# A gate group ahead of the last unit's transposes, and three value weight units behind the token mixes

## The chip, the cores and the metric

The kernel runs on one core of a Trainium2 chip. The metric is the device time of one execution in microseconds; several executions are taken and their median is compared.

## What is computed

Three layers run one after the other: hashed attention, a gated feed-forward block with token shift, and a spatial gating block. Cut to what matters:

```
q_bucket, k_bucket = bits of (q @ proj > 0), (k @ proj > 0)       # 2 x 8 heads, 768 tokens, 64 wide
scores = where(q_bucket == k_bucket, q @ k.T / 8, -1e9)
x = softmax(scores) @ v                                            # heads side by side: 2 x 768 x 512

xk = mu_k * x + (1 - mu_k) * x_prev                                # x_prev: one token earlier
xr = mu_r * x + (1 - mu_r) * x_prev
k = relu(xk @ w_k);  r = sigmoid(xr @ w_r)
x = r * (k * k @ w_v)                                              # w_k 512x1024, w_v 1024x512, w_r 512x512

h = relu(x @ w_in);  u, v = halves of h
out = (u * (w_spatial @ layernorm(v) + b_spatial)) @ w_out
```

The change touches only the order in which the end of the attention and the first half of the second layer are issued.

## The kernel before

**Attention.** Two heads form a pair, eight pairs in all. A *unit* is one strip of 128 queries of one head: its scores (`scores`, L326, 128x768), the clamped copy and row maximum on VectorE (`peak`, L336), the exponential on ScalarE (`expo`, L354), and then `move` for each half: three transposes on TensorE (L364) and the evacuation into PT on ScalarE (L370). There are 96 units. `av3` multiplies PT by v (L399), and `finish` scales the sum on VectorE by the reciprocals (L411), which `recip` and `spread` take through two small DMAs on the SP queue (L385, L392). Three units form a step p, 32 steps in all.

**Mixers.** The second layer works on four blocks of 384 tokens. For block n, `mix_jobs` makes each of four channel slots from x and x shifted: a product `d` (L144 on ScalarE, or L146 on VectorE), a sum `f` on VectorE (L150), a rounded half on ScalarE (L121), and the remainder on VectorE or POOL (L122). Every operand is held in two parts, so a product is three matmuls. `mm3` (L176) makes a *group*: four channels by three matmuls, 12 matmuls of 128x384. `r_group(n, m)` is one gate group with its sigmoid; four make r(n). `step_k` makes eight key groups (relu, square and split on ScalarE, remainder on VectorE, L600). `step_v` multiplies them by the value weights, chunk after chunk for block 0. The order is r(0), k(0), r(1), r(2), r(3), v(0), k(1), v(1) and so on.

**Weights.** A weight unit is 128 rows by 512 columns; it comes by DMA into one of two staging buffers (`w_raw`, L37) as 64-bit words and is turned into two parts by eight jobs: magnitude (ScalarE, L41), clamp, shift, top (VectorE, L44, L49, L55), first (ScalarE, L71), power, low (VectorE, L62, L65), and rest (two instructions on VectorE for the value weights, L76 and L77). w_v has eight units.

**What sets the order.** The order on each engine is written out by the program. In the attention, jobs hang on the places of a step. From the last steps on there are *turns*: `tick()` is called after each group (and once for four pieces of `step_v`) and issues the jobs planned for that turn. Turn 0 is the first gate group; k(0) has turns 4 to 11, r(1), r(2) and r(3) turns 12 to 23, and v(0) begins behind. `plan_weight(n, ...)` puts a unit's load at turn n - 2 and its jobs at turns n to n + 3. Value units 0 and 1 begin in the attention, and only their last jobs have turns. The mixes of block 1 have turns 4 to 8, those of block 2 turns 11 to 14, of block 3 turns 15 to 18. An engine works strictly in its own order, so a job that has to wait holds up all behind it.

Of the kernel before, what the change touches and what calls it, by code (L numbers as in the profile page):

```python
# [82 lines left out]
def hash_attention_moe_kernel(  # L83
# [134 lines left out]
    with tc.manual_schedule():  # L218
        attention(**env)
        mixers(**env)  # L220


def attention(tc, nc, mid, dram, ident, msc, omu, misc, cst_sb, pb, epsT, kq, vP, XT, TK0, wr, w_r, wk,
              w_k, w_v, ps_s, ps_t, obank, mix_jobs, r_group, tick, now, at_tick, plan_weight, wv, **_):
    PS = bass.MemoryType.PSUM
    with ExitStack() as ctx:
# [89 lines left out]
        def scores(i):  # L316
            g, u = divmod(i, 6)
            pp, half = divmod(g, 2)
            e, j = divmod(u, 3)
            t = TK[pp % 2][e]  # L320
            q0 = half * HS + 128 * j
            s = ps_s.tile([128, 2, 512], F32, tag="s", name="s")
            for n in range(2):
                w = t[:, 3 - n, q0:q0 + 128]
                for c in range(2):
                    nc.tensor.matmul(  # L326
                        s[:, c, :HS], w, t[:, n, c * HS:(c + 1) * HS],
                        start=(n == 0), stop=(n == 1),
                    )
            S_ps[i] = s  # L330
# [16 lines left out]
        def expo(i):  # L347
            g, u = divmod(i, 6)
            c, nb = C_sb.pop(i)
            if u == 0:  # L350
                den[g] = at.tile([128, 6], F32, tag="den", bufs=2, name="den")
                PT[g] = mid.tile([128, 2, 6, HS], F32, tag="PT", bufs=2, name="PT")
            c = c.rearrange("p c n -> p (c n)")
            nc.scalar.activation(  # L354
                c, c, AF.Exp, bias=nb, scale=0.125, accum_out=den[g][:, u:u + 1]
            )
            P[i] = c

        def transp(i, c):
            p = P[i] if c == 0 else P.pop(i)  # L360
            t = ps_t.tile([128, 512], F32, tag="t", name="t")
            for n in range(3):
                k0 = 128 * (3 * c + n)
                nc.tensor.transpose(t[:, 128 * n:128 * n + 128], p[:, k0:k0 + 128], ident)  # L364
            return t

        def evac(i, c, t):
            g, u = divmod(i, 6)
            e, j = divmod(u, 3)
            nc.scalar.copy(  # L370
                PT[g][:, e, 3 * c:3 * c + 3, 128 * j:128 * j + 128],
                t[:, :HS].rearrange("p (n q) -> p n q", n=3),
            )
# [3 lines left out]
        def recip(g):  # L377
            rc = rcs[g % 2]
            nc.vector.tensor_scalar_add(rc[:, 0:6], den.pop(g), 1e-9)
            nc.vector.reciprocal(rc[:, 0:6], rc[:, 0:6])  # L380
            rt = at.tile([128, 32], F32, tag="rt", bufs=2, name="rt")
            nc.vector.transpose(rt, rc)
            ds = dram.tile([6, 128], F32, tag="ds", name="ds")
            for n in range(4):
                nc.sync.dma_start(ds[:, 32 * n:32 * n + 32], rt[32 * n:32 * n + 6, :])  # L385
            R[g] = ds

        def spread(g):
            ds = R[g]
            R[g] = at.tile([128, 3, 128], F32, tag="rb", bufs=2, name="rb")  # L390
            for e in range(2):
                nc.sync.dma_start(  # L392
                    R[g][64 * e:64 * e + 64],
                    ds[3 * e:3 * e + 3].unsqueeze(0).to_broadcast([64, 3, 128]),
                )
# [11 lines left out]
        def finish(g):  # L407
            pp, half = divmod(g, 2)
            b, p = divmod(pp, NP)
            PT.pop(g)  # L410
            nc.vector.tensor_mul(  # L411
                XT[:, p, b, 1 + half * HS:1 + (half + 1) * HS],
                obank[:, :HS],
                R.pop(g).rearrange("p n q -> p (n q)"),
            )
# [3 lines left out]
        early = {}  # L419
# [15 lines left out]
        def plan_wv():  # L435
            for h in range(2):
                wv.append(mid.tile([128, 2, 4, DM], F32R, tag="PT", bufs=2, name="wv"))
                for c in range(4):
                    n = 4 * h + c
                    if n < 2:  # L440
                        at_tick(n, early[n][4])
                        at_tick(n + 1, early[n][7])
                        continue
                    plan_weight(
                        (20 * n) // 7 - 2, (wv[h][:, 0, c, :], wv[h][:, 1, c, :]),
                        w_v[128 * n:128 * n + 128],
                    )

# [61 lines left out]
        def av3(p):  # L510
            for n in range(3):
                av(p // 2, 3 * (p % 2) + n)

        def move(i, c):
            evac(i, c, transp(i, c))

        def score(i):
            peak(i)
            bias(i)

        for p in range(np3):
            a = 3 * p
            scores(a)
            scores(a + 1)
            score(a)
            if a:
                move(a - 1, 0)
            expo(a)
            if a:
                move(a - 1, 1)  # L530
            score(a + 1)
            expo(a + 1)
            if p >= 3:
                av3(p - 3)
            if p >= 2 and p % 2 == 0:
                recip(p // 2 - 1)
            for job in plan.pop((p, 0), ()):
                job()
            if p >= 3 and p % 2:
                spread((p - 3) // 2)  # L540
            if p >= np3 - 2:
                tick()
            scores(a + 2)
            move(a, 0)
            move(a, 1)
            score(a + 2)
            expo(a + 2)
            if p >= 4 and p % 2 == 0:
                finish((p - 4) // 2)
            move(a + 1, 0)  # L550
            move(a + 1, 1)
            for job in plan.pop((p, 1), ()):
                job()
            if p == np3 - 2:
                plan_wv()
            if p >= np3 - 2:
                tick()
        move(nunits - 1, 0)
        move(nunits - 1, 1)
        av3(np3 - 3)  # L560
# [1 line left out]
            for job in plan.pop((np3, k), ()):  # L562
                job()
        recip(np3 // 2 - 1)
        r_group(0, 0, mid)
        finish(np3 // 2 - 2)
        r_group(0, 1, mid)
        spread(np3 // 2 - 1)
        av3(np3 - 2)
        av3(np3 - 1)  # L570
# [309 lines left out]
```

## Time and profile before

| | |
|---|---|
| median of 3 runs | 573.2 us (572.47 to 573.58) |
| profiled execution | 572.43 us, span 570.7 us |
| TensorE busy | 548.7 us, 96% of the span |
| VectorE busy | 378.0 us, 66% |
| ScalarE busy | 336.4 us, 59% |
| POOL busy | 143.2 us, 25% |
| mean granted TensorE clock | 0.988 of full speed |

Times in the profile are microseconds from the start of the span. TensorE is busy nearly all the time; a share of busy time says nothing of whether it ran at full clock, so the row of granted clock is read beside it.

### The profile page before, as it was taken

How to read it: one execution, taken by the hardware profiler on the slowest of the kernel's cores; microseconds unless marked ns; L12 is line 12 of the kernel's file. 1: busy time of each engine (PE TensorE's matmuls, PEld its weight loads, DVE VectorE, ACT ScalarE, POOL GpSimd, SP SyncE). 2: the span in 40 equal slices, each digit the busy share in tenths (PEclk: the TensorE clock that was granted, in tenths of full speed). 3: DMA queues.
4: the chain of work that ended last, by engine and by line, in shares of the span. 5: the costliest groups of instructions: out<-in, count | busy, mean ns of one | idle time of the engine just before them, and what ended most of it. 6: DMA issues, size and time to landing. Idle time of an engine off the chain costs nothing.

```text
span 570.7 us, 8997 instructions
## 1 busy us (share of the span) xinstructions
PE 548.7 (96%) x3188; PEld 468.0 (82%) x3188; DVE 378.0 (66%) x812; ACT 336.4 (59%) x718; POOL 143.2 (25%) x152
## 2 busy tenths in 40 slices
PE   7899999999999998799899999999999999999997
PEld 5676767667667765589799999999999889899996
DVE  6678887888688989439974676423997785353230
ACT  2987978798888887539754564808534453221121
POOL 5766663858293822200000000000110000000000
PEclk9999999999999999799899999999999999999999
DMA  8993589393939220202220121000473100001102
GB/s 171 240 223 87 157 152 221 86 237 78 235 90 211 76 89 14 89 0 75 74 75 2 37 74 37 2 1 0 127 253 119 51 33 1 2 14 43 55 20 92
DMA packets 20477, 51.96 MB, mean 91 GB/s; under 512 B 3840, under 2 KB 6864, under 8 KB 20432
## 3 DMA queue, kind: packets, MB, share of 16 engines
q1 hardware_dynamic: 13952, 31.71, 17.9%
q0 software_dynamic: 6336, 19.66, 16.9%
q8 instruction: 25, 0.41, 0.3%
q14 instruction: 20, 0.16, 0.1%
q10 hardware_dynamic: 144, 0.02, 0.0%
HBM read 47.08 MB, written 3.19 MB: 88 GB/s over the span
## 4 chain that ended last, share of the span: by engine, by line
PE 76%; DVE 14%; ACT 5%; issue 3%; DMA 2%; SPq 0%; POOL 0%; DVEq 0%; ACTq 0%; POOLq 0%
PE o L176 11%; PE o L399 9%; PE t L364 8%; PE v L634 8%; PE s L326 8%; PE k L176 7%; PE s L176 7%; PE w L176 5%; PE u L176 5%; PE r L176 4%; DVE p L336 4%; PE o L634 3%; DVE w_a L65 2%; ACT p L354 2%; DVE f L150 2%
## 5 line engine op out<-in xcount | busy, mean ns | idle before, releaser
L336 DVE TENSOR_SCALAR_CACHE_REDUCE p<-s 128x768 f32<-128x768 f32 x96 | 91.6, 954 | 26.9 <-PE s L326 24.2
L354 ACT ACTIVATE p<-p,nb 128x768 f32<-128x768 f32 x96 | 90.4, 942 | 18.8 <-DVE nb L344 18.5
L370 ACT COPY PT<-t 128x384 f32<-128x384 f32 x192 | 84.0, 475 | 19.9 <-PE t L364 18.9
L326 PE MATMUL s<-tk 128*128 128x384 f32 x384 | 84.8, 354 | 4.3 <-DVE p L336 2.2
L364 PE MATMUL t<-ident,p 128*128 128x128 f32 x576 | 80.4, 279 | 8.4 <-ACT p L354 5.7
L326 PEld LDWEIGHTS s<-tk 128*128 128x128 f32 x384 | 63.7, 188 | 24.3 <-issue 4.9
L364 PEld LDWEIGHTS t<-ident,p 128*128 128x128 f32 x576 | 65.6, 142 | 20.4 <-ACT p L354 10.1
L399 PE MATMUL o<-PT,v 128*64 128x384 f32 x384 | 70.7, 506 | 0.0
L176 PE MATMUL k<-tk,wk 128*128 128x384 f32 x336 | 59.6, 334 | 0.0
L258 POOL TENSOR_TENSOR tk<-x,tk 64x384 fp32r<-64x384 f32 x56 | 58.9, 1077 | 2.3 <-DMA tk<-in_kq_dram 0.8
L176 PEld LDWEIGHTS k<-tk,wk 128*128 128x128 f32 x336 | 58.4, 188 | 0.0
L634 PE MATMUL v<-k,wv 128*128 128x384 f32 x288 | 53.8, 335 | 0.6 <-DVE k L600 0.6
L634 PEld LDWEIGHTS v<-k,wv 128*128 128x128 f32 x288 | 50.3, 188 | 0.9 <-DVE k L600 0.9
L399 PEld LDWEIGHTS o<-PT,v 128*64 128x64 f32 x384 | 25.2, 139 | 29.6 <-issue 28.2
L693 POOL DMA_DIRECT2D wsp<-in_w_spT_dram x6 | 3.6, 612 | 179.0 <-DVE w_a L44 172.5
L176 PE MATMUL r<-tk,wr 128*128 128x384 f32 x168 | 34.3, 361 | 2.3 <-DVE tk L122 1.7
L176 PEld LDWEIGHTS r<-tk,wr 128*128 128x128 f32 x168 | 31.8, 204 | 5.5 <-DVE tk L122 2.3
L176 PE MATMUL o<-wk,tk 128*128 128x512 f32 (+1 forms) x168 | 36.2, 374 | 0.0
L176 PEld LDWEIGHTS o<-wk,tk 128*128 128x128 f32 x168 | 30.0, 188 | 5.5
L615 ACT ACTIVATE kr<-k 128x384 f32<-128x384 f32 x28 | 13.6, 487 | 33.0 <-PE k L176 32.8
L600 DVE TENSOR_TENSOR k<-kt,k 128x384 fp32r<-128x384 f32 x32 | 17.8, 555 | 22.2 <-ACT k L618 22.0
L176 PE MATMUL w<-wk,tk 128*128 128x512 f32 x132 | 30.7, 390 | 0.0
(108 smaller groups left out, 846.4 us busy)
## 6 DMA issues: line engine op xcount, KB each, us to landing
tk<-in_kq_dram POOLq DMA_DIRECT2D x32, 384.0 KB, 9.4
x<-in_kq_dram POOLq DMA_DIRECT2D x6, 768.0 KB, 6.6
w_raw<-in_w_k_dram SPq DMA_DIRECT2D x8, 512.0 KB
w_raw<-in_w_v_dram SPq DMA_DIRECT2D x8, 512.0 KB
w_raw<-in_w_in_dram SPq DMA_DIRECT2D x8, 512.0 KB
v<-in_vP_dram SPq DMA_DIRECT2D x8, 384.0 KB
rb<-ds SPq DMA_DIRECT2D x32, 96.0 KB
out_dram<-ot SPq DMA_DIRECT2D x11, 256.0 KB
```

Source lines behind the costliest of these rows:

```text
L65: nc.vector.scalar_tensor_tensor(st["a"].bitcast(F32), st["raw"][:, :, 0], 2.0 ** -52, st["p"].bitcast(F32), op0=ALU.mult, op1=ALU.mult,)
L176: nc.tensor.matmul(o, a, x, start=(i == 0), stop=(i == len(seq) - 1))
L258: nc.gpsimd.tensor_sub(tk[l, 1 + 2 * t, o], raw[pp][l, t, o], tk[l, 2 * t, o])
L326: nc.tensor.matmul(s[:, c, :HS], w, t[:, n, c * HS:(c + 1) * HS], start=(n == 0), stop=(n == 1),)
L336: nc.vector.tensor_scalar(c, s[:, :, :HS], -BIG / 2, None, op0=ALU.max, op1=ALU.max, accum_out=m)
L354: nc.scalar.activation(c, c, AF.Exp, bias=nb, scale=0.125, accum_out=den[g][:, u:u + 1])
L364: nc.tensor.transpose(t[:, 128 * n:128 * n + 128], p[:, k0:k0 + 128], ident)
L370: nc.scalar.copy(PT[g][:, e, 3 * c:3 * c + 3, 128 * j:128 * j + 128], t[:, :HS].rearrange("p (n q) -> p n q", n=3),)
L399: nc.tensor.matmul(obank[64 * e:64 * e + 64, :HS], vt[g // 2][:, kt, e, :], PT[g][:, e, kt, :], start=(kt == 0), stop=(kt == 5),)
L600: later(lag, lambda: eng.tensor_sub(lo, src, hi))
L615: nc.scalar.activation(r, o[:, :HS], AF.Relu)
L634: nc.tensor.matmul(os[m][:, :HS], w, x, start=(c == 0 and k == 0), stop=(c == 7 and k == 2),)
```

## The change

`attention` now issues the first gate group before the last unit's two `move` calls, and the second one where the first two stood (one ahead of `finish` in place of two around it). As the first group is also turn 0, all that hangs on turns 0 and 1 is issued at other places. The jobs of value units 0 and 1 are given one turn more. The turns of units 2 to 7, which were 3, 6, 9, 12, 15, 18, become 2, 5, 8, 16, 19, 22.

```diff
                     if n < 2:
-                        at_tick(n, early[n][4])
-                        at_tick(n + 1, early[n][7])
+                        at_tick(n + 1, early[n][4])
+                        at_tick(n + 2, early[n][7])
                         continue
                     plan_weight(
-                        (20 * n) // 7 - 2, (wv[h][:, 0, c, :], wv[h][:, 1, c, :]),
+                        (0, 0, 2, 5, 8, 16, 19, 22)[n], (wv[h][:, 0, c, :], wv[h][:, 1, c, :]),
                         w_v[128 * n:128 * n + 128],
                     )
...
+        r_group(0, 0, mid)
         move(nunits - 1, 0)
         move(nunits - 1, 1)
         av3(np3 - 3)
         for k in range(2):
             for job in plan.pop((np3, k), ()):
                 job()
         recip(np3 // 2 - 1)
-        r_group(0, 0, mid)
+        r_group(0, 1, mid)
         finish(np3 // 2 - 2)
-        r_group(0, 1, mid)
         spread(np3 // 2 - 1)
         av3(np3 - 2)
         av3(np3 - 1)
```

On TensorE, at the end of the attention (t are transposes, o<-PT,v is av3, r the gate groups; each x12 of r is one group):

```order
 L326 MATMUL s<-tk_1_88 128x384 x4
-L364 MATMUL t<-ident,p 128x128 x18
-L399 MATMUL o_70<-PT,v 64x384 x6
-L176 MATMUL r<-tk_0_77,wr 128x384 x24
+L364 MATMUL t<-ident,p 128x128 x12
+L176 MATMUL r<-tk_0_77,wr 128x384 x12
+L364 MATMUL t<-ident,p 128x128 x6
+L399 MATMUL o_70<-PT,v 64x384 x6
+L176 MATMUL r<-tk_0_77,wr 128x384 x12
 L399 MATMUL o_70<-PT,v 64x384 x12
 L176 MATMUL r<-tk_0_77,wr 128x384 x24
```

The first gate group moved from behind the last six transposes and the av3 to between the last six transposes and the twelve before them.

On ScalarE, at the same place (PT<-t are evacuations, rg<-r the sigmoid of a gate group), before:

```order
L370 COPY PT<-t 128x3x128 x2
L121 CAST tk_1_78<-f 128x384
L214 ACT_TABLE_LOAD
L214 ACTIVATE rg<-r 128x384
L71 CAST wv<-w_b 128x512
```

and now:

```order
L214 ACT_TABLE_LOAD
L214 ACTIVATE rg<-r 128x384
L370 COPY PT<-t 128x3x128 x2
L121 CAST tk_1_78<-f 128x384
L214 ACTIVATE rg<-r 128x384
```

The table load and the first sigmoid moved ahead of the last unit's two evacuations and the last cast of the key mix.

On VectorE, in the gate blocks (tk_1 is the mix of block 2, tk_0 behind it that of block 3; w_a, w_b, w_p and wv are value weight units), before:

```order
L122 TENSOR_TENSOR tk_1_78<-f,tk_1_78 128x384
L150 SCALAR_TENSOR_TENSOR f<-XT,msc,d 128x384 x2
L44 TENSOR_SCALAR w_a<-w_a 128x512
L49 TENSOR_SCALAR w_a<-w_a 128x512
L55 SCALAR_TENSOR_TENSOR w_b<-w_raw,w_a 128x512
L122 TENSOR_TENSOR tk_1_78<-f,tk_1_78 128x384 x2
L150 SCALAR_TENSOR_TENSOR f<-XT,msc,d 128x384
L62 TENSOR_SCALAR w_p<-w_b 128x512
L65 SCALAR_TENSOR_TENSOR w_a<-w_raw,w_p 128x512
L122 TENSOR_TENSOR tk_1_78<-f,tk_1_78 128x384
```

and now:

```order
L122 TENSOR_TENSOR tk_1_78<-f,tk_1_78 128x384
L150 SCALAR_TENSOR_TENSOR f<-XT,msc,d 128x384 x2
L122 TENSOR_TENSOR tk_1_78<-f,tk_1_78 128x384 x2
L150 SCALAR_TENSOR_TENSOR f<-XT,msc,d 128x384
L122 TENSOR_TENSOR tk_1_78<-f,tk_1_78 128x384
L150 SCALAR_TENSOR_TENSOR f<-XT,msc,d 128x384
L122 TENSOR_TENSOR tk_0_77<-f,tk_0_77 128x384
L150 SCALAR_TENSOR_TENSOR f<-XT,msc,d 128x384 x2
L44 TENSOR_SCALAR w_a<-w_a 128x512
L49 TENSOR_SCALAR w_a<-w_a 128x512
L55 SCALAR_TENSOR_TENSOR w_b<-w_raw,w_a 128x512
```

Value unit 5 moved from between the pieces of block 2's mix to between those of block 3's; units 6 and 7 now stand behind both.

## Rows read from the trace of the kernel before

**Rows 1.** The page, 40 slices of 14.27 us: TensorE's busy share and granted clock, tenths.

```profile
PE   7899999999999998799899999999999999999997
...
PEclk9999999999999999799899999999999999999999
```

**Rows 2.** Timeline, 233 to 242: start, us, engine, line, operation, [idle before <-releaser].

```profile
233.88 1.54 PE L364 MATMUL t<-ident,p 128*128 128x128 f32 x6 [2.89 <-ACT p L354]
...
234.46 0.52 ACT L121 CAST tk<-f 128x384 fp32r<-128x384 f32 x1
...
234.87 1.06 ACT L370 COPY PT<-t 128x384 f32<-128x384 f32 x2
...
236.36 1.28 ACT L214 ACT_TABLE_LOAD   x1
...
241.95 0.49 ACT L214 ACTIVATE rg<-r 128x384 f32<-128x384 f32 x1 [4.30 <-PE r L176]
```

**Rows 3.** Stretches: busy time (instructions) of each engine, granted clock, DMA share.

```profile
233.00:235.00 2.00, 1.12 (x6) 1.12 (x6) 1.22 (x5) 2.00 (x6) 0.00 (x0) 0.50 0.00 0
...
256.76:276.36 19.60, 19.60 (x115) 19.60 (x114) 19.06 (x36) 18.18 (x38) 0.00 (x0) 1.00 0.24 82
...
281.00:283.00 2.00, 1.76 (x6) 0.90 (x4) 1.97 (x5) 1.65 (x4) 0.00 (x0) 0.50 0.00 0
```

**Rows 4.** The chain of waits: start, us, engine, tile, line, instructions.

```profile
209.07 0.91 PE t L364 x6
209.98 2.09 PE o L399 x12
...
235.42 4.04 PE o L399 x12
239.46 4.54 PE r L176 x24
244.00 4.02 PE o L399 x24
248.02 4.36 PE r L176 x24
...
291.89 2.08 PE o L176 x12
...
300.21 1.07 PE v L634 x6
```

**Rows 5.** Timeline of the gate blocks, 276 to 297.

```profile
276.36 0.61 DVE L150 SCALAR_TENSOR_TENSOR f<-XT,msc,d 128x384 f32<-128x384 f32 x1
...
278.45 0.44 PE L176 MATMUL r<-tk,wr 128*128 128x384 f32 x1 [0.59 <-ACT tk L121]
...
278.78 0.61 ACT L144 ACTIVATE d<-XT,omu 128x384 f32<-128x384 f32 x1
...
280.32 2.29 PE L176 MATMUL r<-tk,wr 128*128 128x384 f32 x6 [1.43 <-DVE tk L122]
...
282.25 0.55 DVE L122 TENSOR_TENSOR tk<-f,tk 128x384 fp32r<-128x384 f32 x1
...
282.85 9.04 PE L176 MATMUL r<-tk,wr 128*128 128x384 f32 x38 [0.24 <-DVE tk L122]
...
296.16 0.69 DVE L77 TENSOR_TENSOR wv<-w_b,w_a 128x512 fp32r<-128x512 f32 x1
```

**Rows 6.** Instruction groups, VectorE, 256.7 to 282.8: count | busy us, mean ns.

```profile
L65 DVE SCALAR_TENSOR_TENSOR w_a<-w_raw,w_p 128x512 f32<-128x512 uint32 x4 | 2.8, 692 | 0.1
...
L55 DVE SCALAR_TENSOR_TENSOR w_b<-w_raw,w_a 128x512 uint32<-128x512 uint32 x3 | 2.1, 693 | 0.1
L62 DVE TENSOR_SCALAR w_p<-w_b 128x512 uint32<-128x512 uint32 x4 | 1.7, 420 | 0.0
L49 DVE TENSOR_SCALAR w_a<-w_a 128x512 uint32<-128x512 uint32 x3 | 1.3, 427 | 0.1
L44 DVE TENSOR_SCALAR w_a<-w_a 128x512 f32<-128x512 f32 x3 | 1.3, 421 | 0.0
```

## The prediction

> **What bounds the kernel now.** I read the page first: TensorE is busy for 96% of the span (the table of the profile), with less than 9 tenths, but for the first two slices and the last, only in slices 16, 17 and 20, and the clock it was granted falls visibly in slice 17 alone [rows 1]. A change that removes nothing can gain only where TensorE stands idle or runs at a low clock, so these places are where to look; a slice of 14.27 us can hide a short fall, and the table by shorter stretches has a second one in slice 20. The two places are those that the diff touches: the end of the attention (about 231 to 240 us) and the gate blocks (about 277 to 289 us). I then read the timeline, the table by stretches and the chain of waits of both.
>
> *End of the attention.* The last unit's transposes start at 233.88; TensorE was idle for the 2.89 us before that, waiting for ScalarE's exponential of that unit [rows 2]. From 233 to 235 us the granted clock was 0.50, the lower of the two levels, 1.2 GHz [rows 3]. In the chain six transposes took 1.54 us and the attention-times-value step (av3) behind them 4.04 us; earlier the same pieces took 0.91 and 2.09 us [rows 2, 4]. So the gap costs twice, as idle time and as slow work behind it.
>
> *Gate blocks.* After k(0), the eight key groups of block 0, twelve groups make gates (r(1), r(2), r(3), four each). In the first group of r(2) TensorE stops three times, for 0.59, 1.43 and 0.24 us, each time for ScalarE's or VectorE's half of a token-mix slot [rows 5]; the clock is 0.50 in 281 to 283 [rows 3]. VectorE is what is late: in the 19.60 us from the first token mix it worked for 19.06 [rows 3]. It carries three things at once there: the mixes, the key blocks' remainders, and the value weight units.
>
> **The change, part by part.** All sums are against the profiled execution, 572.43 us (span 570.7 and 1.73 around it). The median of the runs is 573.2, which is 0.77 more.
>
> *Part 1: the first gate group goes into the gap.* r(0) group 0 reads mix slots and weights that were finished long before, and writes a score buffer whose unit VectorE has already read, so it can start when TensorE falls idle, at 233.88 - 2.89 = 230.99. A group of 12 matmuls takes 2.08 us at full clock [rows 4], so it ends near 233.1 and leaves about 0.8 us of idle time. The transposes still start at 233.88, since nothing ahead of the exponential is moved on VectorE or ScalarE. If the clock then stays up, the rest is: 6 transposes 0.91, av3 2.09, r(0) group 1 2.08, two av3 4.02, two r groups 4.36 [rows 4] = 13.46 us, so k(0) starts at 247.34. Before it started at 248.02 + 4.36 = 252.38. Gain **5.04 us**: 2.08 for the moved group; 0.63 on the transposes (1.54 - 0.91), 1.95 on the av3 (4.04 - 2.09), and 0.38 on the gate groups (4.54 - 2 x 2.08), these three being the clock's.
>
> What pays for it: ScalarE now loads its table (1.28 us) and does a sigmoid (0.49) ahead of the last two evacuations (1.06 together) [rows 2]. From 234.98 (end of the cast that begins at 234.46) that is 234.98 + 1.28 + 0.49 + 1.06 = 237.8. Their first reader is the second av3, which TensorE reaches at 233.88 + 0.91 + 2.09 + 2.08 = 238.96. So 1.15 us of cover is left and I cost it at nothing; if it were gone, TensorE would wait by as much as the cover is short. On SP the load of value unit 2 moves ahead of the four small transfers of the last reciprocals. Its staging buffer was released when unit 0's remainder was formed, well before the load is reached, so it does not block that queue: cost nothing. The POOL queue is unchanged. The loads of units 5 to 7 go back by four turns with their units; behind them on SP stand only the loads of w_in, whose first unit is not touched before turn 29, in the value block: cost nothing, and if that cover were gone the key groups of block 1 would not wait for it either, since they read other weights.
>
> *Part 2: units 5, 6, 7 behind the mixes.* Ahead of the last VectorE half of r(2)'s mix, unit 5's clamp, shift, top, power and low are gone: 0.42 + 0.43 + 0.69 + 0.42 + 0.69 = 2.65 us [rows 6]. Unit 2's power and low (1.11 us) now run before k(0)'s first remainder, in time VectorE had free. Two bounds follow for the wait in r(2). If VectorE's stream simply closes up, the last half, which ended at 282.81, that is 30.43 us after k(0)'s start, comes at 30.43 - 3.76 = 26.7 us; TensorE asks for it after 12 groups and nine and a bit matmuls, 24.96 + 1.56 + 0.17 = 26.7: no wait. But with the weight work out of the way the ping-pong between ScalarE and VectorE over one product buffer shows. In the trace the second slot's sum started at 276.36 and ScalarE's last product ended at 279.39, 3.03 later [rows 5]; behind that come sum 0.62, cast 0.52, remainder 0.55 and three handovers of about 0.04, together 4.8. The second slot's sum started 23.98 after k(0); less 1.11, and with up to 0.62 back because ScalarE's cast of unit 2 now stands ahead of the first product, it starts at about 23.2. The last half then ends at 28.0, a wait of 1.3 us. I take 1.3, as the handovers are rows; the ends are 0 and 2.
>
> The same for r(3): VectorE has four sums, four remainders and five ops of unit 5 to do, 4 x 0.62 + 4 x 0.55 + 2.65 = 7.3 us, plus handovers, 1.3 as in r(2) (4.8 less three sums and three remainders) and about 0.6 for the first slot behind a sigmoid: 9.2, ending at 37.2. TensorE, 1.3 late, asks for it at 33.28 + 1.3 + 1.73 = 36.3: a wait of 0.9, with ends 0 and 2. That is what is late next, and the old kernel never saw it because TensorE arrived later.
>
> So from k(0) to the first value matmul: 20 groups x 2.08 = 41.6 and 2.2 of waits = 43.8 us. Before: 300.21 - 252.38 = 47.83. Gain **4.0 us** (between 2.2 and 6.2). The loss of 6.2 before is 2.26 of stops and 3.97 at the low clock.
>
> *Sum.* 5.04 + 4.0 = 9.0 us. Nothing is added, and behind the gate blocks all work follows TensorE's order as before. 572.43 - 9.0 = 563.4 for the profiled execution; for the median 573.2 - 9.0 = **564.2 us**.
>
> **A rule weighed.** Six transposes took 0.91 us in one place and 1.54 in the other [rows 2, 4]: transposes run at either level, and most of what TensorE did just before the gap was transposes. The Trainium skill (TensorE: Matmul & The Clock Gate, Part 4: PE-mode transpose) says that the full clock does not engage for transposes. By that, a piece of matmuls set between transposes might not hold the clock, and the sum would be 9.0 less the clock's share. The trace speaks against the strict form, since the attention is full of transposes and shows 9 tenths or more up to slice 16 [rows 1]; rival 2 carries what is left of it.
>
> **The rivals.**
> 1. *The clock falls once more in the gate blocks.* Stops of 0.59 and 1.43 us close together were followed by 0.50 before [rows 3, 5]; I leave stops of about 1.3 and 0.9. For: they are of the same kind. Against: they are shorter and 8 us apart. Price: the 3.97 us that the low clock cost there, at most; about 3.7. Gain 5.3, time 567.9.
> 2. *The clock falls at the end of the attention all the same.* Part 1 then yields only the moved group: 9.0 - 2.96 (0.63 + 1.95 + 0.38) = 6.0, time 567.2. For: 0.8 us of idle time stays, with transposes on both sides. Against: the gap shrinks from 2.89 to a third.
> 3. *ScalarE takes VectorE's place in the gate blocks and part 2 gains nothing:* 573.2 - 5.0 = 568.2. For: it was busy for 18.18 of the same 19.60 us [rows 3]. Against: it too loses two ops of unit 5.
> 4. *Slower: the value block waits for the last unit.* It is consumed chunk by chunk, and unit 7 is chunk 7. It was complete at 296.85 [rows 5], 44.5 us after k(0)'s start; four turns later, at 2.08 each, that is 52.8. Chunk 7 is asked for at 43.8 + 7 x 2.08 = 58.4. It has 5.6 us to spare; the kernel gets slower only if unit 7 comes over 5.6 + 9.0 = 14.6 us later than that, through its load (two staging buffers, each freed by the unit two before). At 16 us it would be 574.6. Nothing in the trace is that late.
> That the change does not do what it says is excluded by the order of instructions.
>
> **How the numbers follow.** Forecast 0.62 (waits from 0 to 4 us: 562.0 to 566.0), rival 1 0.18, rival 2 0.10, rival 3 0.06, rival 4 0.03, and 0.01 for no change. The range from 561.8 to 568.2 takes in the forecast, rivals 2 and 3, and the likelier half of rival 1. About 0.2% is what a measurement of this kernel can tell from no change. Faster by more 0.96, within it 0.01, slower 0.03.
>
> **What would show it.** Right: a gate group at about 231 to 233, the last transposes still near 233.9 taking 0.9 us, the clock at 1.00 from 229 to 245, k(0) at about 247.3, first value matmul near 291, with two waits for mix halves of about a microsecond. Wrong: 0.50 in either place; a wait of the second av3 for the evacuations (cover overestimated); a first value matmul later than 296 (part 2 gave nothing); TensorE waiting in the value block for a weight (rival 4).

## The result, and the profile after

| | before | changed |
|---|---|---|
| median, first comparison | 573.39 us | 565.76 us |
| ratio, with its 95% interval | | 0.9863 (0.9832 to 0.9895) |
| median, second comparison (below) | 572.66 us | 565.10 us |
| ratio, with its 95% interval | | 0.9863 (0.9832 to 0.9893) |
| profiled execution | 572.43 us, span 570.7 | 565.32 us, span 563.5 |
| mean granted clock in it | 0.988 | 0.999 |

The change makes the kernel faster by 1.4%, about 7.9 us by the ratio (6.0 to 9.6); the medians themselves differ by 7.6 us. The forecast was 564.2 us, a gain of 9.0.

The page of the changed kernel; the first row is the span, the others answer to [rows 1]:

```profile
span 563.5 us, 8998 instructions
...
PE   7799999999999998899999999999999999999997
...
PEclk9999999999999999999999999999999999999999
```

The seventeenth slice now shows 9 tenths of granted clock where it showed 7, and TensorE's busy share is 8 in slices 16 and 17. The stretches of two microseconds (busy time of each engine, granted clock, DMA share), the end of the attention and the gate blocks, answer to [rows 3]:

```profile
233.00:235.00 2.00, 1.37 (x8) 1.05 (x7) 1.86 (x5) 0.90 (x2) 0.00 (x0) 1.00 0.00 0
235.00:237.00 2.00, 1.82 (x12) 1.11 (x14) 0.64 (x4) 1.98 (x6) 0.64 (x1) 1.00 0.06 13
281.00:283.00 2.00, 2.00 (x14) 2.00 (x13) 1.88 (x4) 2.00 (x6) 0.00 (x0) 1.00 0.00 0
```

The granted clock is 1.00 in both places. The timeline of the end of the attention answers to [rows 2]:

```profile
232.04 2.33 PE L176 MATMUL r<-tk,wr 128*128 128x384 f32 x12
...
235.18 0.91 PE L364 MATMUL t<-ident,p 128*128 128x128 f32 x6 [0.81 <-ACT p L354]
...
236.30 1.28 ACT L214 ACT_TABLE_LOAD   x1
...
237.60 0.49 ACT L214 ACTIVATE rg<-r 128x384 f32<-128x384 f32 x1
237.98 0.86 ACT L370 COPY PT<-t 128x384 f32<-128x384 f32 x2
...
240.41 4.09 PE L399 MATMUL o<-PT,v 128*64 128x384 f32 x24
```

The gate group runs in the gap, 232.04 to about 234.4, and 0.81 us of the 2.89 us of idle time are left. The last transposes take 0.91 us in place of 1.54. ScalarE's table load, sigmoid and two evacuations end at 238.84, and the av3 that reads the evacuated halves starts at 240.41: the cover (the time between the two) was 1.57 us, where the prediction counted on 1.15. The chain of waits, from the av3 to k(0), and the first value matmul, answers to [rows 4]:

```profile
236.09 2.08 PE o L399 x12
238.18 2.30 PE r L176 x12
240.48 4.02 PE o L399 x24
244.50 4.36 PE r L176 x24
248.87 8.32 PE k L176 x48
...
293.11 1.06 PE v L634 x6
```

From the last transposes to k(0) it is 248.87 - 235.18 = 13.69 us, against 252.38 - 233.88 = 18.50 before: 4.81 gained. From k(0) to the first value matmul it is 293.11 - 248.87 = 44.24, against 47.83: 3.59 gained. The two together are 8.40. What stands behind the first value matmul is the same in both: 570.7 - 300.21 = 270.5 and 563.5 - 293.11 = 270.4. What stands ahead differs by 1.30 us the other way, though TensorE's work is the same up to there, but for the gate group in the gap: the last transposes started at 233.88 before and at 235.18 now. The chain at the start shows where that comes from, first the kernel before, then the changed one:

```profile
14.58 4.89 DMA x<-in_kq_dram
```

```profile
14.28 6.54 DMA x<-in_kq_dram
```

The load of the second pair's keys and queries (x) took 4.89 us in the one execution and 6.54 in the other. 8.40 - 1.30 = 7.1, and the spans differ by 7.2. Among the profiled executions of this study the last transposes start between 233.8 and 235.8 us, whatever the kernel, so stages are compared below and not spans.

What is left of the waits in the gate blocks, in the timeline of both mixes (answers to [rows 5]):

```profile
269.35 0.61 ACT L144 ACTIVATE d<-XT,omu 128x384 f32<-128x384 f32 x1
...
272.17 0.62 DVE L150 SCALAR_TENSOR_TENSOR f<-XT,msc,d 128x384 f32<-128x384 f32 x1
...
274.60 0.61 ACT L144 ACTIVATE d<-XT,omu 128x384 f32<-128x384 f32 x1
...
276.49 0.56 DVE L122 TENSOR_TENSOR tk<-f,tk 128x384 fp32r<-128x384 f32 x1 [0.63 <-ACT tk L121]
...
276.51 0.44 PE L176 MATMUL r<-tk,wr 128*128 128x384 f32 x1 [0.51 <-ACT tk L121]
...
277.11 6.86 PE L176 MATMUL r<-tk,wr 128*128 128x384 f32 x38 [0.15 <-DVE tk L122]
...
285.65 0.55 DVE L122 TENSOR_TENSOR tk<-f,tk 128x384 fp32r<-128x384 f32 x1
...
286.25 0.62 PE L176 MATMUL o<-tk,wr 128*128 128x384 f32 x2 [0.55 <-DVE tk L122]
```

### The profile page after: what moved, and what is told of

Same layout as the page of the kernel before. It is cut to its first block, busy times and chain, and to the rows that moved or that the text cites. A ratio compares the mean times of both kernels' runs of the same rounds, so it can differ in the third digit from the quotient of the medians.

```text
span 563.5 us, 8998 instructions
## 1 busy us (share of the span) xinstructions
PE 544.1 (97%) x3188; PEld 464.9 (82%) x3188; DVE 378.4 (67%) x812; ACT 336.1 (60%) x718; POOL 143.2 (25%) x152
## 4 chain that ended last, share of the span: by engine, by line
PE 76%; DVE 12%; ACT 6%; DMA 3%; issue 2%; SPq 0%; POOL 0%; ACTq 0%; DVEq 0%; POOLq 0%
PE o L176 11%; PE o L399 8%; PE v L634 8%; PE s L326 8%; PE t L364 8%; PE k L176 8%; PE s L176 7%; PE w L176 5%; PE u L176 5%; DVE p L336 4%; PE o L634 3%; PE r L176 2%; DVE f L150 2%; ACT p L354 2%; DVE w_a L65 2%
## 5 line engine op out<-in xcount | busy, mean ns | idle before, releaser
L399 PE MATMUL o<-PT,v 128*64 128x384 f32 x384 | 68.8, 494 | 0.0
L176 PE MATMUL r<-tk,wr 128*128 128x384 f32 x168 | 31.4, 339 | 0.8 <-ACT tk L121 0.5
L176 PEld LDWEIGHTS r<-tk,wr 128*128 128x128 f32 x168 | 29.0, 188 | 3.1 <-ACT tk L121 1.1
```

Of the source, the lines that this page charges most:

```text
L176: nc.tensor.matmul(o, a, x, start=(i == 0), stop=(i == len(seq) - 1))
L399: nc.tensor.matmul(obank[64 * e:64 * e + 64, :HS], vt[g // 2][:, kt, e, :], PT[g][:, e, kt, :], start=(kt == 0), stop=(kt == 5),)
```

## The experiments

The theory: the gain is the sum of two stages, each by its own mechanism. At the end of the attention a filled gap keeps the clock up; in the gate blocks VectorE reaches the mixes earlier. The rivals: the clock falls whatever fills the gap, or only for some kinds of work; the parts lean on each other; ScalarE is the bound in the gate blocks; something behind gives a part back.

In the table the stages are read from TensorE's timeline in each profile, whose rows start up to 0.17 us ahead of the chain's: A from the start of the last transposes to that of k(0), B from there to the first value matmul, C from there to the end of the span.

| | median us | ratio to before (95%) | A | B | C |
|---|---|---|---|---|---|
| before | 573.16, 572.66 | | 18.34 | 47.83 | 270.65 |
| changed | 565.76 | 0.9863 (0.9832 to 0.9895) | 13.52 | 44.25 | 270.55 |
| changed again | 565.10 | 0.9863 (0.9832 to 0.9893) | 13.53 | 44.28 | 270.65 |
| part 1 alone | 569.02 | 0.9923 (0.9896 to 0.9950) | 13.53 | 47.94 | 270.65 |
| part 2 alone | 568.94 | 0.9930 (0.9905 to 0.9955) | 17.25 | 44.27 | 270.65 |
| gap filled, matmuls | 571.19 | 0.9973 (0.9956 to 0.9990) | 15.60 | 47.35 | 270.62 |
| gap filled, transposes | 570.70 | 0.9954 (0.9939 to 0.9969) | 15.60 | 47.38 | 270.60 |
| sums in place | 563.76 | 0.9837 (0.9808 to 0.9866) | 13.53 | 42.47 | 270.56 |
| four units late | 563.10 | 0.9826 (0.9797 to 0.9855) | 13.50 | 41.96 | 270.58 |
| both of these | 562.47 | 0.9817 (0.9788 to 0.9845) | 13.52 | 41.60 | 270.57 |

(The first median of before, 573.16, goes with the four runs of parts and filled gaps, the second with the last four.)

### Part 1 alone

```diff
-                        (0, 0, 2, 5, 8, 16, 19, 22)[n], ...
+                        (20 * n) // 7 - 2, ...
```

(against the changed kernel)

> Part 1 alone: the gate group ahead of the last transposes, value units 2 to 7 on their old turns 3, 6, 9, 12, 15, 18. Theory (the two parts add up): the end of the attention takes 13.7 us from the last transposes to k(0) as in the changed kernel, against 18.5 before, a gain of 4.8; the gate blocks still take about 47.8 us from k(0) to the first value matmul, with the low clock in them. Time 573.4 - 4.8 = 568.6. Rival (the parts lean on each other: starting k(0) earlier only makes VectorE later in the gate blocks): the wait there grows by up to 4.8 and the time stays near 573.

A is the changed kernel's, B the kernel before's, with the clock at 0.50 in it. One stretch of the gate blocks:

```profile
281.00:283.00 2.00, 2.00 (x8) 2.00 (x8) 1.93 (x6) 1.03 (x2) 0.00 (x0) 0.50 0.24 96
```

The gain is 4.4 us by the ratio (2.9 to 6.0). k(0) started as early as in the changed kernel (248.77 us in the chain, 248.87 there), and the gate blocks took as long as in the kernel before, so VectorE's lateness moved with k(0). The rival, that the parts lean on each other, is out; the gains of the two parts alone, 4.4 here and 4.0 below, add up to 8.4.

### Part 2 alone

```diff
-                        (20 * n) // 7 - 2, ...
+                        (0, 0, 2, 5, 8, 16, 19, 22)[n], ...
```

(against the kernel before)

> Part 2 alone: the new turns 2, 5, 8, 16, 19, 22, the gate group left where it was. Theory: the end of the attention as before, 18.5 us with the clock at 0.50; the gate blocks about 44.2 us as in the changed kernel, a gain of 3.6. Time 573.4 - 3.6 = 569.8. Rival (ScalarE, not VectorE, is the bound in the gate blocks and the gain there came with part 1): the gate blocks keep 47.8 us and the time 573.

B is 44.27, as in the changed kernel, while the gate group still stands behind the av3. So it is the units' place that frees the gate blocks, and ScalarE does not take VectorE's place. By the ratio the gain is 4.0 us (2.6 to 5.4). A came out otherwise than expected, 17.25 in place of 18.34. Up to the first sigmoid TensorE, VectorE and ScalarE have the same order of work there as in the kernel before:

```profile
234.93 0.91 PE t L364 x6
235.84 3.57 PE o L399 x12
239.41 4.54 PE r L176 x24
...
252.34 8.32 PE k L176 x48
```

Here the clock fell later behind the same gap of 2.89 us: the transposes ran at 0.91 us, and the av3 took 3.57, not 4.04. So the price of the fall is not one number, and the profile that the prediction was made from shows the larger of these two. Its mean clock, 0.988, lies inside what the 34 executions of the kernel before show that were run beside the experiments, 0.979 to 0.994; which falls these had is not known.

### The gap filled with matmuls that nobody reads

```diff
+        fill = ps_s.tile([128, 2, 512], F32, tag="s", name="fill")
+        for n in range(12):
+            nc.tensor.matmul(fill[:, 0, :HS], wr[:, n % 2, n % 4, :128],
+                             TK0[0][:, n % 4, :HS], start=(n == 0), stop=(n == 11))
         move(nunits - 1, 0)
```

(against the kernel before)

> The kernel before, with twelve more matmuls of 128x384 in the gap ahead of the last transposes, whose result nobody reads; nothing is moved. This separates the clock from the moved work. Theory (work in the gap holds the clock): the granted clock stays at 1.00, the pieces behind take 13.4 + 2.1 us, and the time falls by 2.96 us to 570.4 though TensorE has 2.08 us more to do. Rival (the gap's worth is only the moved group, the clock falls anyway): no change, 573.4.

TensorE's timeline (its last row is cut off by the end of the window), and two stretches with the granted clock:

```profile
230.68 2.33 PE L560 MATMUL fill<-tk,wr 128*128 128x384 f32 x12
233.83 0.91 PE L364 MATMUL t<-ident,p 128*128 128x128 f32 x6 [0.82 <-ACT p L354]
234.67 2.16 PE L399 MATMUL o<-PT,v 128*64 128x384 f32 x12
...
249.43 1.89 PE L176 MATMUL k<-tk,wk 128*128 128x384 f32 x10
```

```profile
233.00:235.00 2.00, 1.18 (x9) 0.82 (x10) 1.19 (x4) 2.00 (x6) 0.00 (x0) 1.00 0.00 0
235.00:237.00 2.00, 2.00 (x13) 0.82 (x10) 0.13 (x1) 1.98 (x4) 1.83 (x2) 1.00 0.06 13
```

The clock stays at 1.00 and A falls to 15.60, 2.74 below the kernel before's profile, although TensorE does 2.08 us more (forecast: 13.4 + 2.1 = 15.5). By the ratio the gain is smaller, 1.5 us (0.6 to 2.5). Against part 2 alone, with its shorter fall, A is 17.25 - 15.60 = 1.65 lower; that falls of both lengths are mixed in the ratio would explain it, and was not shown. The moved work gives the other part of the gain in A: 15.60 - 13.52 = 2.08, one gate group exactly.

### The gap filled with transposes

```diff
+        fill = ps_s.tile([128, 2, 512], F32, tag="s", name="fill")
+        for n in range(14):
+            k0 = 128 * (n % 3)
+            nc.tensor.transpose(fill[:, 0, k0:k0 + 128], PT[15][:, 0, n % 3, :128], ident)
         move(nunits - 1, 0)
```

(against the kernel before)

> The same with fourteen transposes of 128x128 (about 2.1 us) in place of the twelve matmuls. Theory (transposes are work like any other for the clock, since the attention is full of them at full clock): clock 1.00 and 570.4 as with matmuls. Rival (the full clock does not engage for transposes): the clock falls to 0.50 behind the gap and the time stays at 573.4.

```profile
231.96 1.69 PE L561 MATMUL fill<-ident,PT 128*128 128x128 f32 x14
235.02 0.91 PE L364 MATMUL t<-ident,p 128*128 128x128 f32 x6 [1.37 <-ACT p L354]
235.86 2.16 PE L399 MATMUL o<-PT,v 128*64 128x384 f32 x12
...
250.62 1.55 PE L176 MATMUL k<-tk,wk 128*128 128x384 f32 x8
```

```profile
233.00:235.00 2.00, 0.65 (x6) 0.41 (x4) 1.75 (x5) 1.06 (x3) 0.00 (x0) 1.00 0.00 0
235.00:237.00 2.00, 1.98 (x14) 1.23 (x16) 0.57 (x3) 2.00 (x6) 0.80 (x1) 1.00 0.06 13
```

Fourteen transposes fill 1.69 us, less than the matmuls and less than the 2.1 expected, and leave 1.37 us idle; from 229.83 to 235.9 TensorE does nothing but transposes. The clock stays at 1.00 all the same, A is 15.60 again, and the ratio says 2.6 us (1.8 to 3.5). So here transposes held the clock as matmuls did. In both profiles in which the gap stands open (the kernel before and part 2 alone) the clock fell behind it; in the eight in which it is filled it is 1.00 from 229 us to k(0).

### The change again, and the waits that it leaves

> The changed kernel once more, for a narrower size. Theory (the stages tell the gain: 4.8 at the end of the attention and 3.6 in the gate blocks, and the load of the first pair varies alike in both kernels): 8.4 us below the kernel before, ratio 0.9853. Rival (something behind the gate blocks gives a part back, as the first median of 7.6 could mean): 7.6 or less, ratio 0.987 or more.

The ratio came out the same to four digits, 7.9 us with the same width, and the medians again differ by 7.6: the times do not tell 8.4 from 7.6. In the profiled executions the stages tell it: A falls by 4.8 and B by 3.6 once more, and C is 270.55 to 270.65 in all profiles, so there nothing is given back behind the gate blocks.

Two edits take what is left of B. The first writes a product into the sum's buffer, with three such buffers:

```diff
-                st["d"] = pool.tile([128, HS], F32, tag="d", bufs=1, name="d")
+                st["d"] = st["f"] = pool.tile([128, HS], F32, tag="f", bufs=fbufs, name="f")
...
-                st["f"] = pool.tile([128, HS], F32, tag="f", bufs=fbufs, name="f")
```

(with fbufs 3, and the two tiles of `step_s` that share these buffers taken from the same three)

> The changed kernel with the product of a mix written into the sum's own buffer, of which there are three, in place of one product buffer: ScalarE can make a product while VectorE still reads the one before. Theory (what is left of the waits is the hand-over over the one buffer): the last half of r(2)'s mix comes about 1 us earlier, TensorE loses 0.7 us there in place of 1.7 and 0.3 in r(3) in place of 0.9, the gate blocks take 42.6 us, and the time is 1.6 below the changed kernel. Rival (VectorE's amount of work sets it): gate blocks 44.2 us, same time.

B is 42.47, the forecast within 0.13: the hand-over over one product buffer was worth 1.8 us. (The edit has three buffers for products and sums together, as there were before, one and two; sharing them and writing in place were not separated.) The second moves unit 4 behind the mixes too:

```diff
-                        (0, 0, 2, 5, 8, 16, 19, 22)[n], ...
+                        (0, 0, 2, 5, 18, 20, 22, 24)[n], ...
```

> The changed kernel with value unit 4 also behind the mixes: turns 18, 20, 22, 24 for units 4 to 7. Theory (VectorE's and ScalarE's weight work ahead of the mixes sets the waits): 4.1 us of VectorE's and 1.3 of ScalarE's work go, the first product of r(2)'s mix comes at 19.2 us after k(0)'s start in place of 20.5, its last half about 1.3 us earlier, r(3)'s wait vanishes, the gate blocks take about 42.0 us and the time is 2.2 below the changed kernel. Rival (the last unit comes too late for the value block): TensorE waits in v(0) for a value weight and the gain is given back there.

```profile
268.53 0.61 ACT L144 ACTIVATE d<-XT,omu 128x384 f32<-128x384 f32 x1
...
275.29 0.56 DVE L122 TENSOR_TENSOR tk<-f,tk 128x384 fp32r<-128x384 f32 x1 [0.64 <-ACT tk L121]
...
275.90 6.54 PEld L176 LDWEIGHTS r<-tk,wr 128*128 128x128 f32 x38 [0.40 <-DVE tk L122]
...
290.92 1.23 PE L634 MATMUL v<-k,wv 128*128 128x384 f32 x6
```

The first product of r(2)'s mix starts 268.53 - 249.12 = 19.4 us after k(0), where the changed kernel has 269.35 - 248.87 = 20.5, and its last remainder ends at 275.85, 26.7 us after k(0), against 28.2. TensorE still waits for one mix half for some tenths; in the value block it waits for no weight. The last unit is complete at 302.65, and by 2.08 us a chunk its chunk is asked for at 290.92 + 7 x 2.08 = 305.48, so about 2.8 us are to spare. B is 41.96.

> Both together. Theory: no wait for a mix is left, the gate blocks take 41.6 to 41.8 us with the clock at 1.00, 2.5 us below the changed kernel. Rival (one of the two already takes all there is): no better than the better one of them.

```profile
229.00:250.00 21.00, 19.89 (x118) 14.89 (x117) 10.93 (x22) 10.56 (x22) 3.16 (x3) 1.00 0.12 36
250.00:290.00 40.00, 40.00 (x233) 40.00 (x232) 30.98 (x58) 32.27 (x68) 0.00 (x0) 1.00 0.13 42
```

From 250 to 290 us TensorE is busy without a gap, and B is 41.60, which is 20 groups at 2.08: no wait is left. The two edits alone took 1.8 and 2.3 us off B, together 2.7, so they partly remove the same wait. Against the changed kernel's 565.10 us the three medians are 1.3, 2.0 and 2.6 lower; 1.6, 2.2 and 2.5 were expected. The last is the fastest version of the study, 562.47 us. Its interval and that of four units late overlap; the order of the two rests on B.

## Why the prediction was right

**What bounds the kernel:** right. Both places were the ones where time came out; behind them C stayed within 0.1 us, and what differs ahead of them starts at a load (4.89 and 6.54 us).

**Part 1:** right in mechanism. The parts of its sum: the moved group 2.08 (measured 15.60 - 13.52 = 2.08); transposes 1.54 to 0.91 and av3 4.04 to 2.08, as foretold. The gate group by itself in the chain took 2.30 us where the sum had 2.08: 13.69 in place of 13.46. The sum gave the whole 0.38 us of the two gate groups (4.54 - 2 x 2.08) to the clock, but in the chain of the kernel with matmuls in the gap, at full clock, the same two groups still took 4.39. Only 0.15 was the clock's, and its share was 0.63 + 1.95 + 0.15 = 2.73 in place of 2.96; the filled gap measured 18.34 - 15.60 = 2.74. The cover of the evacuations held.

**The clock's share of part 1 was sized from one execution.** There the low clock took the transposes, the av3 and a piece of a gate group. With the same order of work, part 2 alone lost 1.1 us less in A, so against such an execution part 1 would give less than the 4.8 us that the two profiles show. What is shown of the miss, 9.0 forecast and 7.9 measured, is the 0.2 above and the 0.4 below, which take the sum to the 8.4 of the stages. The rest, 0.5, could come from shorter falls, but it is argued and not shown: how often the fall is long and how often short was not measured, the interval of the 7.9 holds 8.4 and 9.0 too, and part 1 alone gave 4.4 with an interval that holds 4.8.

**Part 2:** right in mechanism and order, with both waits where they were expected. The second slot's sum of r(2)'s mix started at 272.17, 23.3 us after k(0) (forecast 23.2), ScalarE's last product ended 3.04 later (3.03), the last remainder ended at 277.05, 28.2 us after k(0) (forecast 28.0), that of r(3) at 286.20, 37.3 after it (forecast 37.2). The waits were sized at 1.3 and 0.9, together 2.2; B has 44.24 - 41.6 = 2.6 us over its bare groups. The missing 0.4 lies in r(2). Twelve groups and ten matmuls behind k(0)'s first matmul, at 248.70 + 24.96 + 1.73 = 275.39, TensorE could have used the last half; it went on at 277.11, 1.72 us later, where the sum had 1.3. About 0.2 of this is the half itself (28.2 for 28.0), and 0.17 is that the sum counted TensorE's 26.7 from k(0)'s start in the chain, which lies 0.17 behind that of its first matmul in the timeline. In r(3) the same working gives 286.25 - (283.80 + 1.73) = 0.72 late, and about 0.1 is lost again at the start of the next group after each of the two waits. The hand-over over the one buffer, which the prediction chose over the closing up of VectorE's stream, is shown by the run in place. It is not the only way to end the wait: with unit 4's work moved too, B fell by 2.3 with the one buffer left as it was.

The title and the heading of part 2 say that three units go behind the mixes. Only units 6 and 7 stand behind both; unit 5 stands among the pieces of r(3)'s mix, and the prediction's sum for r(3) counts it there.

**Rival 1 (a fall in the gate blocks):** in neither profile of the changed kernel. For executions without a trace only the mean clock of the whole run is known, 0.994 to 1.00, and that does not say where a fall was; the second profile of the changed kernel (mean 0.996) shows one at the very start, 0.50 from 17 to 19 us.

The price of this rival was read too high. The prediction split the 6.2 us that were lost in the gate blocks before into 2.26 of stops and 3.97 at the low clock. In the kernel with matmuls in the gap the gate blocks had a shorter fall, and longer stops at the end of the wait:

```profile
279.13 0.44 PE L176 MATMUL r<-tk,wr 128*128 128x384 f32 x1 [0.45 <-ACT tk L121]
280.06 8.28 PE L176 MATMUL r<-tk,wr 128*128 128x384 f32 x38 [0.49 <-DVE tk L122]
```

Two stretches, the first of that kernel, the second of the kernel before, which is still at 0.50 later on:

```profile
282.00:284.00 2.00, 2.00 (x10) 2.00 (x9) 1.93 (x5) 0.93 (x2) 0.00 (x0) 0.72 0.12 49
```

```profile
285.00:287.00 2.00, 2.00 (x8) 2.00 (x7) 1.94 (x4) 0.71 (x2) 0.00 (x0) 0.50 0.02 8
```

Yet its B is 47.35 against 47.83, only 0.48 less. The matmuls behind the last wait start 280.06 - 249.59 = 30.47 us after k(0), and before 282.85 - 252.38 = 30.47: VectorE's last half sets this, and where TensorE ran faster it waited longer (0.45 and 0.49 us, where the kernel before shows 0.24). So slow matmuls ahead of a late half cost nothing of their own. By the prediction's own figures TensorE asks at 26.7 and went on at 30.5: about 3.8 of the 6.2 us were the wait, and about 2.4, worked out and not measured, the clock behind it.

**Rival 2 (the clock falls all the same):** out, by the two filled gaps and by the profile. The rule of the Trainium skill (TensorE: Matmul & The Clock Gate, Part 4: PE-mode transpose), that the full clock does not engage for transposes, would have left the clock at 0.50 behind the gap filled with transposes; it was 1.00 there, in the rows from 233 to 237 us, with fp32 transposes.

**Rival 3 (ScalarE takes over):** out, by part 2 alone. **Rival 4 (a late value weight):** out. The last unit was complete at 296.90, 48.0 us after k(0) where the prediction allowed for 52.8. Even with four units late TensorE waited for no weight in the value block, though only about 2.8 us were then to spare.

## What to carry to other kernels

A gap ahead of work that cannot start earlier is worth more than its idle time when the clock falls behind it, and work that was ready anyway is the cheapest filling; even work that nobody reads paid here (1.5 and 2.6 us by the ratio). Where an operand is late, as in the gate blocks here, a low clock ahead of it adds nothing to the wait: price a fall by the work behind it. When an engine off the critical path is late, look at what its queue holds ahead of the late instruction, and move what has slack behind it: the freedom was in the weights' deadline, not in the mixes. Size a fall of the clock from several executions, and compare stages rather than spans when a load at the start makes them differ by more than a part of the effect.

## What was not expected

The same gap, 2.89 us in both, was followed by a low clock that began ahead of the transposes in one execution (0.50 from 233 us, the transposes at 233.88) and under the av3 in another (av3 3.57 us). At the start of some executions the clock fell too, as in four units late:

```profile
14.00:16.00 2.00, 1.17 (x4) 1.14 (x4) 1.93 (x6) 1.01 (x2) 1.95 (x6) 0.50 0.60 154
```

Six of the ten profiles show it. In them the last transposes start at 234.93 to 235.84 us, in the other four at 233.83 to 235.18; the load of keys and queries varies as well, so what the fall costs there was not separated. A, B and C begin long behind it.
